# A 2-D Fourier mixing and maxout feed-forward kernel: the work before its first matrix products put in another order

## The chip, the cores and the metric

The kernel runs on one core of a Trainium2 chip. The metric is the device time of one execution in microseconds (us), lower is better. A few terms: TensorE (PE) multiplies matrices and writes to PSUM; VectorE (DVE), ScalarE (ACT) and GpSimd (POOL) work elementwise, and DVE and ACT clear PSUM ("eviction"); SP only issues DMAs, ACT and POOL also do. Each engine takes its instructions strictly in order.

## The reference

```python
X = np.fft.fft(np.fft.fft(x, axis=1), axis=2).real      # x: 8 x 3072 x 256
t = X.reshape(24576, 256)
h = np.maximum(np.maximum(t @ w1, t @ w2), t @ w3)      # 256 -> 768
out = h @ w_out                                         # 768 -> 256
```

## The kernel before, in words

**Tiling.** Each of the 8 batches has 3072 rows of 256. The Fourier transform is done as matrix products with tables of sines and cosines. A batch is held as 96 partitions (24 row blocks times 4 column groups) by 128 x 64 elements; a row index `bb` goes from 0 to 127. Products pair row `bb` with row 128-`bb`, so a second, reversed copy of the batch is needed (`reverse`, L125). The mixing of a batch (class `Mix`, L370) has seven stages `s` (L378; 66 products of up to 96 columns, each stage evicted into `z`), six stages `k` (L401; four products of 256 columns with `tabs`, evicted into `t`) and `end` (L421). Then 18 "units" (L687), each a 512-row block by one of six weight chunks: four products `unit_plus` (L427), two `unit_minus` (L437, executed after the next unit's four), and `unit_out` (L444), in which ACT makes a relu and DVE a maximum. The last products (`l2_block`, L461) run ten steps per unit, one block behind.

**Weights.** They are multiplied by the column transform first. `prep_first(jh, ...)` (L324) makes `gE`, `gO` and `gD` for half `jh` of the 768 columns: for each of two weight matrices it yields twice, each time after four products of 384 columns in one PSUM bank. `gE` and `gO` are evicted by copies, `gD` by ACT from the same PSUM bank with the scale `dif` (L341). `prep_second` (L345) makes `g1t` in three steps and `gw` in a fourth.

**The beginning (L156 to L320).** The raw batch 0 comes in six pieces. Rows 80 to 95, 96 to 111 and 112 to 127 are loaded as float32 into `staged` buffers by SP, ACT and SP (L160 to L168), each in four DMAs; the last piece also gets row 128 by `load_next` (L103), eight DMAs, issued after its four. Rows 0 to 31, 32 to 63 and 64 to 79 are loaded by POOL straight into `x0_first` as bfloat16 (L187 to L190). DMAs reuse eight completion counters per path, so a ninth DMA waits for the first to land. POOL writes index vectors first (`iota`, L156), and after the loads it issues the weights (L195, L200).

DVE builds first the small 24-point table (L229 to L263), of which ACT takes sines (L256) and small copies (L268); then the angles of the large table in two parts of 7 and 6 rows (L274 to L282): one pass for the product and three for the reduction to one turn (`_reduce`, L20). ACT takes four passes over each part (L284 to L287: sine, negative sine, absolute value, cosine) into `tabs`. DVE then casts the three `staged` pieces into `x0_first` (L293), and ACT makes the reversed copy `back` (L295, L312; DVE the small part at L313). DVE makes the 256-point angles `vm` (L301 to L309) and ACT their sines `md_all`, `nmd_all` (L310, L311).

**Order by hand.** The schedule is manual: the program's order is each engine's order. PE runs 14 warm-up products on the table (`warm`, L582), the seven `s` of batch 0 (with eviction by ACT, and by DVE for k = 1, 3, 5), `prep_first(0)`, `k0`, one step of `prep_first(1)`, `k1`, another step, and then the units. The dictionary `plan` (L621 to L660) says after which unit each remaining step runs: steps of the weights, the mixing of batch b+1 from unit `begin[b]` on (L640), POOL's reversed copies of the next batches (`turn_chunk`, L134: two casts for each of four chunks) and SP's loads (`fetch`, L635). While `prep_first(0)` and `k` run, the PSUM pool `ps_f` has two banks and `ps_s` six.

Of the kernel before, what the change touches and what calls it, by code (L numbers as in the profile page):

```python
# [9 lines left out]
FP32 = mybir.dt.float32  # L10
# [23 lines left out]
def kernel(  # L34
# [68 lines left out]
    def load_next(eng, dst, b, after=None):  # L103

        xr = x_rows(b)
        for g in range(4):
            for (a0, n, a) in ((0, 23, 1), (23, 1, 0)):
                ld = eng.dma_start(out=dst[g * 24 + a0: g * 24 + a0 + n],
                                   in_=xr[g, a:a + n, 0:1, :])
                if after is not None:  # L110
                    tc.add_manual_dep(ld.ins, after.ins.name, AFTER, reason="weights first")
# [44 lines left out]
    def iota(t, pattern, base=0, cm=0):  # L156
        nc.gpsimd.iota(t, pattern, base=base, channel_multiplier=cm,
                       allow_small_or_imprecise_dtypes=True)

    staged = []  # L160
    for (r0, eng) in ((80, nc.sync), (96, nc.scalar), (112, nc.sync)):
        n = 17 if r0 == 112 else 16
        xs = xs_pool.tile([96, 33 * 64], FP32, name="xs", tag="xs")
        xv = xs[:, 0:n * 64].rearrange("p (bb dl) -> p bb dl", dl=64)
        load_rows(eng, xv[:, 0:16, :], 0, r0, r0 + 16)
        if n > 16:
            load_next(eng, xv[:, 16:17, :], 0)
        staged.append((r0, n, xs))  # L168

    pidx = gen.tile([128, 1], FP32, tag="pidx")  # L170
    iota(pidx, [[0, 1]], cm=1)
    jm24 = gen.tile([96, 48], FP32, tag="jm24")
# [6 lines left out]
    i13 = gen.tile([128, 13], FP32, tag="i13")  # L179
    iota(i13, [[1, 13]])  # L180
    j128 = gen.tile([128, 128], FP32, tag="j128")
    iota(j128, [[24, 128]])
# [3 lines left out]

    x0_first = x0_pool.tile([96, 64 * 130], BF16, name="x0", tag="x0")  # L187
    x0v = x0_first.rearrange("p (bb dl) -> p bb dl", dl=64)
    for (r0, r1) in ((0, 32), (32, 64), (64, 80)):
        load_rows(nc.gpsimd, x0v[:, r0:r1, :], 0, r0, r1)  # L190
# [21 lines left out]
    nc.gpsimd.memset(z[:, :, 24:26], 0.0)  # L212

    consts_of = {}
    for (name, value) in (("half_pi", 0.5 * math.pi), ("rnd", ROUND), ("n24", -24.0),
                          ("n256", -256.0), ("n3072", -3072.0)):
# [3 lines left out]
    s24 = gen.tile([96, 24], FP32, tag="s24")  # L220
    nc.vector.memset(s24[:, 0:13], 6.0)
    nc.vector.memset(s24[:, 13:24], 0.0)
# [5 lines left out]

    ge24 = gen.tile([96, 5], FP32, tag="ge24")  # L229
# [27 lines left out]
    pi13 = gen.tile([128, 13], FP32, tag="pi13")  # L257
    nc.vector.tensor_scalar(out=pi13, in0=i13, scalar1=pidx, scalar2=None, op0=ALU.mult)
# [11 lines left out]
    w = gen.tile([128, 13 * 128], FP32, tag="w")  # L270
    v = gen.tile([128, 13 * 128], FP32, tag="v")
    q = gen.tile([128, 13 * 128], FP32, tag="q")
    turn = float(2.0 * math.pi / 3072.0)
    for (r0, r1) in ((0, 7), (7, 13)):  # L274
        cs = slice(r0 * 128, r1 * 128)
        n = r1 - r0
        nc.vector.scalar_tensor_tensor(
            out=v[:, cs].rearrange("p (r j) -> p r j", j=128),
            in0=j128.unsqueeze(1).to_broadcast([128, n, 128]), scalar=pidx,
            in1=pi13[:, r0:r1].unsqueeze(2).to_broadcast([128, n, 128]),  # L280
            op0=ALU.mult, op1=ALU.add)
        _reduce(nc, w[:, cs], v[:, cs], q[:, cs], 3072.0, consts_of["rnd"], consts_of["n3072"])  # L282
        wr = w[:, cs].rearrange("p (r j) -> p r j", j=128)
        nc.scalar.activation(out=tabs[:, r0:r1, 0, :], in_=wr, func=AX.Sin, scale=turn)  # L284
        nc.scalar.activation(out=tabs[:, r0:r1, 2, :], in_=wr, func=AX.Sin, scale=-turn)
        nc.scalar.activation(out=w[:, cs], in_=w[:, cs], func=AX.Abs)
        nc.scalar.activation(out=tabs[:, r0:r1, 1, :], in_=wr, func=AX.Sin, scale=-turn,  # L287
                             bias=consts_of["half_pi"])

    back = gen.tile([96, 33 * 130], BF16, tag="back")  # L290
    xr0 = back.rearrange("p (dl bb) -> p dl bb", bb=130)
    for (r0, n, xs) in (staged[1], staged[0], staged[2]):
        nc.vector.tensor_copy(out=x0_first[:, r0 * 64:(r0 + n) * 64], in_=xs[:, 0:n * 64])  # L293
    for (r0, n) in ((80, 49), (0, 31), (31, 32)):
        reverse(nc.scalar.copy, xr0, x0_first[:, r0 * 64:(r0 + n) * 64], r0, n)  # L295
# [3 lines left out]
    pf = gen.tile([128, 2], FP32, tag="pf")  # L299
    for fc in range(2):  # L300
        nc.vector.tensor_scalar(out=pf[:, fc:fc + 1], in0=pidx, scalar1=float(128 * fc),  # L301
                                scalar2=None, op0=ALU.add)
# [6 lines left out]
    _reduce(nc, vm, vm, qm, 256.0, consts_of["rnd"], consts_of["n256"])  # L309
    nc.scalar.activation(out=md_all, in_=vm, func=AX.Sin, scale=float(2.0 * math.pi / 256.0))  # L310
    nc.scalar.activation(out=nmd_all, in_=vm, func=AX.Sin, scale=float(-2.0 * math.pi / 256.0))  # L311
    reverse(nc.scalar.copy, xr0, x0_first[:, 63 * 64:80 * 64], 63, 17, 32, 49)  # L312
    reverse(nc.vector.tensor_copy, xr0, x0_first[:, 63 * 64:80 * 64], 63, 17, 49, 65)  # L313
# [10 lines left out]
    def prep_first(jh, evict_e, bank=lambda: ps_f.tile([128, 512], FP32, name="psg", tag="ps")):  # L324

        cs = slice(jh * 384, (jh + 1) * 384)
        for i, wv in enumerate((w2_bf, w3_bf)):
            for half in range(2):
                psg = bank()
                hs = slice(half * 128, (half + 1) * 128)  # L330
                for k, (table, wt) in enumerate(((md, wv), (nmd, w1_bf))):
                    for fc in range(2):
                        nc.tensor.matmul(  # L333
                            psg[:, 0:384], table[fc][:, hs],
                            wt[:, fc * DFF + jh * 384: fc * DFF + jh * 384 + 384],
                            start=(k == 0 and fc == 0), stop=(k == 1 and fc == 1))
                if half == 0:
                    evict_e(out=gE[i][:, cs], in_=psg[:, 0:384])
# [31 lines left out]
    class Mix:  # L370
# [30 lines left out]
        def k(self, q):  # L401
# [15 lines left out]
            nc.scalar.copy(  # L417
# [163 lines left out]
    for _ in range(14):  # L581
        nc.tensor.matmul(warm, tab[:, 4864:4992], tab[:, 4480:4992], start=True, stop=True)  # L582
# [5 lines left out]
    for _ in prep_first(0, nc.scalar.copy):  # L588
        pass
# [7 lines left out]
    second = [prep_first(1, nc.vector.tensor_copy,  # L597
                         lambda: ps_o.tile([128, 512], FP32, name="psg", tag="po")),
# [9 lines left out]

    m.k(0)
    prep_some()  # L610
    m.k(1)
    prep_some()
# [27 lines left out]
    begin = [8, 6] + [5] * (B - 3)  # L640

    for (u, fn) in ((0, prep_some), (1, prep_some),
                    (2, lambda: m.k(2)), (2, prep_some), (3, lambda: m.k(3)),
                    (3, prep_some), (4, prep_some), (5, prep_some),
                    (6, lambda: m.k(4)), (7, lambda: m.k(5)), (7, m.end),
                    (0, lambda: turn_chunk(1, 0)), (2, lambda: turn_chunk(1, 1)),
                    (4, lambda: turn_chunk(1, 2)), (6, lambda: turn_chunk(1, 3))):
        at(0, u, fn)
    for ch in range(4):
        at(0, (3, 5, 7, 9)[ch], lambda ch=ch: fetch(2, ch))  # L650
    for b in range(B - 1):
        for i, whats in enumerate(ahead):
            for what in whats:
                at(b, begin[b] + i, lambda b=b, what=what: piece(b + 1, what))
        if b + 2 < B:
            folds = begin[b] + 8
# [79 lines left out]
```

## Time and profile before

| | us |
|---|---|
| median of 3 runs | 435.25 (434.59 to 435.59) |
| the profiled execution's own time | 436.12 |
| its span, first to last instruction | 434.3 |
| PE busy | 405.1 (93% of the span) |
| DVE, ACT, POOL busy | 273.7, 264.7, 240.1 |
| mean granted TensorE clock | 0.992 |

The profiled execution has 1.8 us outside the span. The page gives for each engine its busy time, then groups of instructions by line; the trace can be asked for rows in order of time: start, duration, engine, line, operation, output<-inputs, and in brackets how long the engine was idle before and what ended that. "x4" is several instructions in one row. PEq, SPq and so on are the sequencers, which issue DMAs.

### The profile page before, as it was taken

What the parts mean: (1) busy time and instruction counts of PE and PEld (TensorE: products, weight loads), DVE (VectorE), ACT (ScalarE), POOL (GpSimd) and SP (SyncE); (2) the same over time, 40 slices, a digit from 0 to 9 for tenths busy, and PEclk for the clock granted to TensorE, in tenths of its full rate; (3) what the DMA queues carried; (4) which work ended last, traced back from release to release, by engine and by line L of the source; (5) the groups of instructions that cost most, each with busy time, mean ns of one, the idle gap of its engine ahead of it and who ended that gap; (6) DMA issues with size and microseconds to landing.
All of it is one profiled execution on the core that took longest, in us unless ns stands there. A gap on an engine that the chain in (4) does not pass through costs nothing.

```text
span 434.3 us, 8699 instructions
## 1 busy us (share of the span) xinstructions
PE 405.1 (93%) x3015; PEld 271.7 (63%) x3070; DVE 273.7 (63%) x449; ACT 264.7 (61%) x486; POOL 240.1 (55%) x288
## 2 busy tenths in 40 slices
PE   0479999998999999999999999999999999999996
PEld 0165666666666666766666666666666666666665
DVE  8724755666656666666656756576656666666773
ACT  3877666665666576656665566656665666754650
POOL 8718522698258922995259823994269812214320
PEclk9969999999999999999999999999999999999999
DMA  9998774176424953188415854186421221111313
GB/s 140 135 180 172 145 185 117 62 188 164 120 74 124 220 115 109 52 205 184 131 50 127 195 121 129 58 197 163 130 76 67 75 62 72 74 50 49 101 72 122
DMA packets 130180, 52.28 MB, mean 120 GB/s; under 512 B 112081, under 2 KB 127192, under 8 KB 130136
## 3 DMA queue, kind: packets, MB, share of 16 engines
q1 hardware_dynamic: 107784, 36.52, 35.3%
q0 software_dynamic: 20624, 14.68, 14.7%
q10 hardware_dynamic: 1728, 0.52, 0.5%
q8 instruction: 24, 0.39, 0.4%
q14 instruction: 20, 0.16, 0.1%
HBM read 29.02 MB, written 25.17 MB: 125 GB/s over the span
## 4 chain that ended last, share of the span: by engine, by line
PE 81%; issue 4%; DVE 4%; POOL 3%; ACT 3%; DMA 3%; DVEq 0%; POOLq 0%; ACTq 0%
PE po L457 26%; PE pse L433 14%; PE pse L441 12%; PE pse L434 11%; PE po L481 3%; PE ps L389 2%; PE ps L387 2%; PE ps L413 2%; PE ps L415 2%; PE pl L473 2%; ACT stmp L447 2%; DMA x<-in_x_dram 2%; DVE ot L486 2%; DVE hm L448 1%; PE psg L333 1%
## 5 line engine op out<-in xcount | busy, mean ns | idle before, releaser
L447 ACT ACTIVATE stmp<-pse 128x512 bf16<-128x512 f32 x288 | 171.1, 600 | 52.4 <-PE pse L434 38.1
L491 POOL DMA_INDIRECT out_dram<-ot,rows_m x92 | 100.3, 1090 | 169.6 <-DVE ot L486 155.2
L448 DVE TENSOR_TENSOR hp<-pse,stmp 128x512 bf16<-128x512 f32 x144 | 99.5, 691 | 130.9 <-ACT stmp L447 95.7
L433 PE MATMUL pse<-t,gE 128*128 128x512 bf16 x287 | 108.8, 379 | 2.6 <-DVE hm L448 0.4
L448 DVE TENSOR_TENSOR hm<-pse,stmp 128x512 bf16<-128x512 f32 x144 | 99.2, 689 | 7.0 <-PE pse L434 3.9
L434 PE MATMUL pse<-t,gO 128*128 128x512 bf16 x256 | 96.9, 379 | 0.1
L457 PE MATMUL po<-wout_bf,hp 128*128 128x256 bf16 x576 | 86.1, 273 | 0.4
L441 PE MATMUL pse<-t,gD 128*128 128x512 bf16 x273 | 82.4, 379 | 0.4
L457 PE MATMUL po<-wout_bf,hm 128*128 128x256 bf16 x576 | 78.5, 273 | 0.3
L457 PEld LDWEIGHTS <-hp 128*128 128x128 bf16 x576 | 56.4, 98 | 26.1
L457 PEld LDWEIGHTS <-hm 128*128 128x128 bf16 x576 | 56.4, 98 | 16.3
L486 DVE TENSOR_TENSOR ot<-po,even 128x512 f32<-128x512 f32 x92 | 62.9, 683 | 0.2 <-PE po L457 0.2
L143 POOL CAST x<-xs 96x1056 bf16<-96x1056 f32 x28 | 56.7, 2025 | 11.1 <-DMA xs<-in_x_dram 11.1
L145 POOL CAST x<-xs 96x1056 bf16<-96x1056 f32 (+1 forms) x35 | 58.1, 1670 | 0.0
L417 ACT CAST t<-ps 128x512 bf16<-128x512 f32 x48 | 28.1, 585 | 43.5 <-PE ps L415 42.2
L394 ACT CAST z_all<-ps 128x480 bf16<-128x480 f32 x45 | 25.1, 558 | 44.3 <-PE ps L389 40.1
L441 PEld LDWEIGHTS <-gD 128*128 128x128 bf16 x288 | 27.9, 98 | 32.2
L434 PEld LDWEIGHTS <-gO 128*128 128x128 bf16 x288 | 28.1, 98 | 21.0 <-issue 3.0
L433 PEld LDWEIGHTS <-gE 128*128 128x128 bf16 x288 | 28.1, 98 | 19.2 <-issue 0.4
L481 PE MATMUL po<-gw,t 128*128 128x512 bf16 x85 | 32.2, 379 | 0.0
L387 PE MATMUL ps<-m24f,x 96*128 96x96 bf16 (+1 forms) x256 | 30.3, 214 | 0.0
L477 ACT COPY even<-pl 128x512 f32<-128x512 f32 x46 | 26.8, 583 | 0.0
(133 smaller groups left out, 326.4 us busy)
## 6 DMA issues: line engine op xcount, KB each, us to landing
xs<-in_x_dram SPq DMA_DIRECT2D x84, 198.0 KB
out_dram<-ot SPq DMA_DIRECT2D x90, 128.0 KB
xs<-in_x_dram SPq DMA_DIRECT2D x28, 192.0 KB
out_dram<-ot,rows_m POOLq DMA_INDIRECT x92, 4.5
w_bf<-in_moe_w_dram POOLq DMA_DIRECT2D x6, 192.0 KB, 6.0
out_dram<-ot SPq DMA_DIRECT2D x17, 64.0 KB
xs<-in_x_dram SPq DMA_DIRECT2D x8, 96.0 KB
x<-in_x_dram POOLq DMA_DIRECT2D x8, 96.0 KB, 8.3
```

What stands on the lines that cost most here:

```text
L143: nc.gpsimd.tensor_copy(v[:, 0:33, ch * 32:ch * 32 + 32], xs[:, 0:32 * 64].rearrange("p (bb dl) -> p dl bb", dl=64)[:, 0:33, :])
L145: reverse(lambda out, in_: nc.gpsimd.tensor_copy(out, in_), v[:, 33:66, :], xs, ch * 32, 33 if ch == 3 else 32)
L387: nc.tensor.matmul(ps1[:, c0:c0 + n], x0[0](d), mf[:, 0:n], start=True, stop=False)
L433: nc.tensor.matmul(pse[:, 0:n], gE[i][:, js], te, start=True, stop=False)
L434: nc.tensor.matmul(pse[:, 0:n], gO[i][:, js], to, start=False, stop=True)
L441: nc.tensor.matmul(pse, gD[i][:, js], to, start=False, stop=True, skip_group_check=True)
L447: nc.scalar.activation(out=stmp[:, 0:n], in_=pses[0][:, 0:n], func=AX.Relu)
L448: nc.vector.tensor_tensor(out=dst, in0=src3, in1=stmp[:, 0:n], op=ALU.max)
L457: nc.tensor.matmul(po, hcols(jc), wout_bf[:, jc * 256:(jc + 1) * 256], start=False, stop=(jc == NJC - 1), skip_group_check=True)
L481: nc.tensor.matmul(po, to[:, cp], gw[:, 256:768], start=True, stop=True)
L486: nc.vector.tensor_tensor(out=ot.rearrange("p (h c) -> p h c", h=2), in0=po.rearrange("p (h c) -> p h c", h=2), in1=lin.unsqueeze(1).to_br ...
L491: stored(nc.gpsimd.indirect_dma_start(out, bass.IndirectOffsetOnAxis(ap=rows_m[0:128 - lo, b * 12 + slot: b * 12 + slot + 1], axis=0), ot[ ...
```

## The change

The reading, the mathematics and the sizes stay. What changes, in the order of the program:

- `load_next` issues five DMAs in place of eight, and for batch 0 it goes ahead of the bulk of rows 112 to 127 on SP.
- POOL writes only `pidx`, `j128` and `i13` before its first four loads of `x0_first`; the other index vectors are put between the loads. The memset of two columns of `z` goes from POOL to DVE.
- The large table comes first on DVE and ACT, and its angles are counted in turns: one product pass and two reduction passes (the first with one source) in place of one and three. ACT makes three passes in place of four; the negative sine is made by DVE (`tab_minus`), for the first seven rows before `vm`, for the last six after all copies. The 24-point table follows.
- `vm` is reduced in two passes in place of three, `half` is set twice, and `nmd_all` is made by DVE from `md_all`.
- ACT reverses the three `staged` pieces straight from float32, before DVE's casts; row pieces 31 to 62 are reversed by DVE. ACT keeps a 48-element strip (which waits for the casts), rows 0 to 30, and half of rows 63 to 79.
- 17 warm-up products in place of 14, on the first rows of the table.
- `prep_first` uses the six-bank pool in the beginning; `gE` is always evicted by DVE, `gD` is made by POOL from `gO`. The order on PE is: seven `s`, two steps of `prep_first(0)`, `k0`, `k1` (evicted by DVE), the other two steps, and then unit 0; the four steps of `prep_first(1)` follow after units 0, 0, 1 and 1.
- The mixing of batch 1 begins after unit 10 in place of 8 (its last seven steps one unit earlier than that would give), two of batch 1's `turn_chunk` go from units 4 and 6 to 5 and 8, the loads of batch 2 from units 3, 5, 7, 9 to 6, 7, 9, 11, and the `turn_chunk` of batch 2 from 16, 18, 20, 22 to 14, 16, 18, 20.

```diff
+        if n > 16:
+            load_next(eng, xv[:, 16:17, :], 0)
         load_rows(eng, xv[:, 0:16, :], 0, r0, r0 + 16)
...
+        nc.vector.tensor_scalar(out=q[:, cs], in0=v[:, cs], scalar1=ROUND, scalar2=None,
+                                op0=ALU.add)
+        nc.vector.scalar_tensor_tensor(out=w[:, cs], in0=q[:, cs], scalar=-ROUND, in1=v[:, cs],
+                                       op0=ALU.add, op1=ALU.subtract)
...
+    tab_angles(0, 7)
+    tab_sines(0, 7)
+    tab_angles(7, 13)
+    tab_sines(7, 13)
...
-    for (r0, n, xs) in (staged[1], staged[0], staged[2]):
-        nc.vector.tensor_copy(out=x0_first[:, r0 * 64:(r0 + n) * 64], in_=xs[:, 0:n * 64])
-    for (r0, n) in ((80, 49), (0, 31), (31, 32)):
-        reverse(nc.scalar.copy, xr0, x0_first[:, r0 * 64:(r0 + n) * 64], r0, n)
+    for (r0, n, xs) in staged:
+        nc.vector.tensor_copy(out=x0_first[:, r0 * 64:(r0 + n) * 64], in_=xs[:, 0:n * 64])
+        reverse(nc.scalar.copy, xr0, xs, r0, n, 32, 64)
+    nc.scalar.activation(out=md_all, in_=vm, func=AX.Sin, scale=float(-2.0 * math.pi / 256.0))
+    for (copy, r0, n, d0, d1) in ((nc.scalar.copy, 80, 49, 64, 65),
+                                  (nc.scalar.copy, 0, 31, 32, 65),
+                                  (nc.vector.tensor_copy, 31, 32, 32, 65),
+                                  (nc.scalar.copy, 63, 17, 32, 49),
+                                  (nc.vector.tensor_copy, 63, 17, 49, 65)):
+        reverse(copy, xr0, x0_first[:, r0 * 64:(r0 + n) * 64], r0, n, d0, d1)
+    nc.vector.tensor_scalar(out=nmd_all, in0=md_all, scalar1=-1.0, scalar2=None, op0=ALU.mult)
+    tab_minus(7, 13)
...
-                    nc.scalar.activation(out=gD[i][:, cs], in_=psg[:, 0:384], func=AX.Copy,
-                                         scale=dif)
+                    nc.gpsimd.tensor_scalar(out=gD[i][:, cs], in0=gO[i][:, cs], scalar1=dif,
+                                            scalar2=None, op0=ALU.mult)
...
-    for _ in prep_first(0, nc.scalar.copy):
+    first = prep_first(0, lambda: ps_s.tile([128, 512], FP32, name="psg", tag="ps"))
+    next(first)
+    next(first)
+    m.k(0)
+    m.k(1, nc.vector.tensor_copy)
+    for _ in first:
         pass
...
-    begin = [8, 6] + [5] * (B - 3)
+    begin = [10, 6] + [5] * (B - 3)
```

More of the change, by code (lines that the diff above doesn't have):

```diff
@@ L105, in load_next @@
         xr = x_rows(b)
[L106 to L111, printed above, removed]
+        parts = [(dst[g * 24: g * 24 + 23], xr[g, 1:24, 0:1, :]) for g in range(4)]
+        parts.append((dst[23:96:24], xr[:, 0, 0:1, :]))
+        for (to, src) in parts:
+            ld = eng.dma_start(out=to, in_=src)
+            if after is not None:
+                tc.add_manual_dep(ld.ins, after.ins.name, AFTER, reason="weights first")
     def load_chunk(b, ch, after=None):
@@ L268 @@
             nc.scalar.activation(out=m[:, o0:o1], in_=src, func=AX.Copy, scale=by)
[L270 to L291, printed above, removed]
-    for (r0, n, xs) in (staged[1], staged[0], staged[2]):
-        nc.vector.tensor_copy(out=x0_first[:, r0 * 64:(r0 + n) * 64], in_=xs[:, 0:n * 64])
-    for (r0, n) in ((80, 49), (0, 31), (31, 32)):
-        reverse(nc.scalar.copy, xr0, x0_first[:, r0 * 64:(r0 + n) * 64], r0, n)
+    tab_minus(0, 7)
     vm = gen.tile([128, 512], FP32, tag="vm")
@@ L308 @@
                                 scalar1=128.0, scalar2=64.0, op0=ALU.mult, op1=ALU.add)
[L309 to L313, printed above, removed]
+    nc.vector.tensor_scalar(out=qm, in0=vm, scalar1=256.0 * ROUND, scalar2=None, op0=ALU.add)
+    nc.vector.scalar_tensor_tensor(out=vm, in0=qm, scalar=-256.0 * ROUND, in1=vm,
+                                   op0=ALU.add, op1=ALU.subtract)
+    back = gen.tile([96, 33 * 130], BF16, tag="back")
+    xr0 = back.rearrange("p (dl bb) -> p dl bb", bb=130)
+    for (r0, n, xs) in staged:
[10 more added lines that the diff above has]
+    tab_minus(7, 13)
     nc.vector.tensor_scalar(out=sgn, in0=pidx, scalar1=0.0, scalar2=None, op0=ALU.is_equal)
@@ L580 @@
     warm = ps_s.tile([128, 512], FP32, name="warm", tag="ps")
-    for _ in range(14):
-        nc.tensor.matmul(warm, tab[:, 4864:4992], tab[:, 4480:4992], start=True, stop=True)
+    for _ in range(17):
+        nc.tensor.matmul(warm, tab[:, 0:128], tab[:, 0:512], start=True, stop=True)
     m = Mix(0)
@@ L653 @@
             for what in whats:
-                at(b, begin[b] + i, lambda b=b, what=what: piece(b + 1, what))
+                at(b, begin[b] + i - (b == 0 and i >= 6), lambda b=b, what=what: piece(b + 1, what))
         if b + 2 < B:
-            folds = begin[b] + 8
+            folds = begin[b] + 8 if b else 14
             for ch in range(4):
```

83 lines of the change are left out of this document (53 added, 30 removed).

## The prediction, written before the changed kernel was run

> **What bounds the kernel now.** I read the table of waits first, for PE alone over the whole span (engine, line, what it waited for, us in total, times, longest).
>
> ```profile
> PE warm L582 <- ACT tab L287: 17.1, 1, 17.1
> PE ps L389 <- ACT back L130: 2.8, 1, 2.8
> PE ps L389 <- POOL x L145: 1.3, 1, 1.3
> ```
>
> PE stands still for 17.1 us, warms up, stands still for 2.8 us more until ACT's reversed copy is done, and after that hardly waits. So the end is set by two things: when the first real product can run, and how fast PE then goes through a fixed list of products. The change touches the first, and a little of the second. Next, the two engines that make what PE waits for, in order of time: first ACT, then DVE.
>
> ```profile
> 4.52 0.28 ACT L256 ACTIVATE t<-v 96x96 f32<-96x96 f32 x1 [0.52 <-DVE v L30]
> ...
> 5.83 0.30 ACT L268 ACTIVATE m0r<-t,ind 96x24 bf16<-96x24 f32 x1
> 9.73 0.95 ACT L284 ACTIVATE tab<-w 128x896 bf16<-128x896 f32 x1 [3.59 <-DVE w L30]
> ...
> 13.63 0.84 ACT L284 ACTIVATE tab<-w 128x768 bf16<-128x768 f32 x1
> ...
> 18.07 6.84 ACT L130 COPY back<-x 96x1568 bf16<-96x1568 bf16 x4 [1.02 <-DVE x L293]
> ```
>
> ```profile
> 1.56 0.65 DVE L230 TENSOR_SCALAR ge<-g,pidx 96x5 f32<-96x5 f32 x1
> ...
> 4.83 0.25 DVE L260 TENSOR_TENSOR m24f<-t,ind 96x96 bf16<-96x96 f32 x1 [0.20 <-ACT t L256]
> ...
> 5.18 1.14 DVE L277 SCALAR_TENSOR_TENSOR v<-j,pidx,pi 128x896 f32<-128x896 f32 x1
> ...
> 9.61 1.01 DVE L277 SCALAR_TENSOR_TENSOR v<-j,pidx,pi 128x768 f32<-128x768 f32 x1
> ...
> 13.52 1.43 DVE L293 CAST x<-xs 96x1024 bf16<-96x1024 f32 x2
> 17.31 0.72 DVE L293 CAST x<-xs 96x1088 bf16<-96x1088 f32 x1 [2.36 <-DMA xs<-in_x_dram]
> 17.96 0.14 DVE L301 TENSOR_SCALAR pf<-pidx 128x1 f32<-128x1 f32 x1
> ...
> 21.94 0.41 DVE L130 COPY back<-x 96x272 bf16<-96x272 bf16 x1
> ```
>
> The reader sees a chain: ACT begins the reversed copy only at 18.07, when DVE has cast the third staged piece, and that piece was late (DVE idle 2.36 us at 17.31). Then four copies in a row take 6.84 us, to 24.91, and the first `s` runs at 24.97. Then PE's clock, by stretches (length, busy PE, PEld, DVE, ACT, POOL, then the granted clock), and three rows of PE in time.
>
> ```profile
> 24.97:30.07 5.10, 5.10 (x65) 5.10 (x66) 1.48 (x3) 3.14 (x6) 0.00 (x0) 0.50 1.04 180
> 30.07:36.26 6.19, 5.85 (x34) 3.47 (x33) 1.05 (x2) 4.21 (x10) 3.99 (x2) 0.91 0.70 158
> 57.52:57.95 0.43, 0.43 (x13) 0.43 (x11) 0.21 (x1) 0.00 (x0) 0.41 (x2) 1.00 0.92 210
> 102.74:106.15 3.41, 3.36 (x34) 2.38 (x36) 1.73 (x3) 1.66 (x4) 2.79 (x3) 1.00 0.58 133
> ```
>
> ```profile
> 39.07 0.49 PE L333 MATMUL psg<-w_bf,md_all 128*128 128x384 bf16 x2
> 39.39 0.49 PE L333 MATMUL psg<-w_bf,nmd_all 128*128 128x384 bf16 x2
> 39.72 0.38 PE L433 MATMUL pse<-t,gE 128*128 128x512 bf16 x1
> ```
>
> All seven `s` of batch 0 run at clock 0.50, in 5.10 us; one `s` of batch 1 takes 0.43 us at 1.00. Four `psg` products take 0.65 us at full clock (39.07 to 39.72). Unit 0 begins where the second stretch ends, at 36.26.
>
> **The change, part by part.** *DVE up to the 24-point table.* A two-source pass over the large table is 4.43/4 = 1.11 us for seven rows (5.18 to 9.61), 6/7 of that for six. The new first reduction pass has one source; the trace has none on float32 alone. The nearest row is the single-source cast, 1.43/2 for 1024 elements, so 0.63 for 896; from the other side it is a full pass, 1.11. I take 0.63. Beginning at about 2.1 (the first small operation of before ends at 2.21), rows 0 to 6 are ready at 2.1 + 1.11 + 0.63 + 1.11 = 4.95, rows 7 to 12 at 7.4. The 24-point chain takes 1.56 to 4.52 = 2.96, so its angles are ready at 10.4.
>
> *ACT.* Four passes took 13.63 - 9.73 = 3.90; three take 2.9 and 2.5. ACT is through at 7.9 and 10.4, takes the sine (0.28) and small copies (to 6.13 from 4.52, 1.6) and is free at about 12.0. Reversed copies cost 6.84 us for 1568 + 48 + 1023 + 1056 = 3695 elements, 1.85 ns each; the three staged pieces, 512, 512 and 544 elements from float32, then take 2.9 us by that row. From above I allow twice, since no row reverses float32. ACT reaches 14.9 and makes `md_all`, then waits for DVE's casts.
>
> *DVE to the end of the casts.* The 24-point products, 4.83 to 5.18, with the wait for ACT end at 11.2; the negative sine of 896 elements is 0.63 by the cast's row (bounds half of it, as both sides are bfloat16, and 1.11), to 11.8. `half` twice, 0.3. The `vm` chain took 21.94 - 17.96 = 3.98; it loses one of three passes of 512 elements (1.11 x 512/896 = 0.63) and 0.27 of another: 3.1, to 15.2. Three casts of 0.72: 17.35.
>
> *The critical end.* ACT's 48-element strip waits for the third cast: 17.7 with its overhead (0.3). Rows 0 to 30: 1023 x 1.85 = 1.9, so 19.6. DVE beside it makes 1056 + 272 elements, by 0.41/272 at most 2.0 us: 19.4. The first `s` runs at about **19.6 instead of 24.97, 5.4 us earlier**. With every unknown at its dear end (three passes 0.48, 0.41 and 0.48 longer, `vm` 0.27) it is 21.2; with the cheap end 19.3. What is late next is that strip behind the casts, and after it the data: the third piece no longer has the small transfers behind it.
>
> ```profile
> 6.45 6.52 SPq L108 DMA_DIRECT2D xs<-in_x_dram  x8
> ```
>
> These eight are issued from 6.45 to 12.97, waiting for counters of bulk loads; now five go out when the first counters are free, and the bulk of rows 112 to 127 goes about 3 us later than before. DVE needs it at 16.6, after two casts. In before DVE waited for the last of the eight until 17.31; the bulk itself had landed before the last of the eight was issued (12.97), so 3 us later is about 16, still ahead of 16.6, so I cost the move at nothing, covered by the `vm` chain. Should it land at 17.3 again, the start is 0.7 later.
>
> *POOL's loads.* Three index vectors fewer stand ahead of them, so each issue comes about 0.9 us earlier; the rows of the last four are needed at about 18.9.
>
> ```profile
> 12.52 0.68 POOL L99 DMA_DIRECT2D x<-in_x_dram  x1 [1.69 <-DMA x<-in_x_dram]
> 13.40 1.06 POOL L99 DMA_DIRECT2D x<-in_x_dram  x1 [0.21 <-issue]
> ```
>
> ```profile
> x<-in_x_dram POOLq DMA_DIRECT2D x4, 48.0 KB, 4.8
> ```
>
> In before the last issue ends at 14.46; with 4.8 us to land, these rows come by 18.4 to 19.3, now up to 0.9 earlier: just hidden. Here the issue beside DVE's casts took 1.06, the one before it, beside two-source passes, 0.68. The Trainium skill, "SBUF — State Buffer", section "Who interferes with whom", says that copies and single-source operations of VectorE in their two-port modes lock GpSimd out for the whole instruction, descriptor writing included, which speaks against the change, since its reduction passes become such. The two rows agree in direction, at 0.38 us per issue that meets one. By the rows that is at most 12 x 0.38 = 4.6 us, below as rival C; in the sum I take nothing, since only three such passes run between 2 and 12 us.
>
> *The clock.* Warm-up starts when the negative sine is written, at 11.8.
>
> ```profile
> 17.11 5.06 PE L582 MATMUL warm<-tab 128*128 128x512 bf16 x14 [17.11 <-ACT tab L287]
> ```
>
> Seventeen take 5.06 plus three at 0.21 to 0.43, so they end at 17.5 to 19.0 and the gap to 19.6 is 0.6 to 2.1 us. In before a gap of 2.8 lost the clock (0.50 from 24.97), a gap of 1.3 did not (1.00 after 102.74). I take it as kept: seven `s` at 0.43 (the last shorter) are 2.8 instead of 5.1, and the 6.19 us at 0.91 that follow hold 0.09 x 6.19 = 0.55 of lost clock: **2.8 us**. The Trainium skill, "TensorE: Matmul & The Clock Gate", "What's actually happening", puts the fall after an idle window of about 3.4 us; the gap of 2.8 above lost it, so the trace is stricter, and by the page rival B would have no chance.
>
> *Between `s` and unit 0.* From 30.07 to 36.26 PE did 24 `psg` (3.9) and two `k` (8 products of 256 columns, by columns 0.87 at 0.65 per 4 x 384) plus the 0.55: 0.87 us were waits for two PSUM banks. Six banks and DVE's share remove about **0.8**; the evictions of `s` keep up, four of them on ACT at 0.56 in 2.8 us.
>
> ```profile
> L394 ACT CAST z_all<-ps 128x480 bf16<-128x480 f32 x45 | 25.1, 558 | 44.3 <-PE ps L389 40.1
> ```
>
> The eight `psg` that move behind units 0 and 1 cost the same there.
>
> *Units.* `gD` on POOL: the fourth one stands behind the two casts of the next batch's first chunk.
>
> ```profile
> 31.88 1.99 POOL L143 CAST x<-xs 96x1056 bf16<-96x1056 f32 x1 [9.14 <-DMA xs<-in_x_dram]
> 33.81 2.06 POOL L145 CAST x<-xs 96x1056 bf16<-96x1056 f32 x1
> ```
>
> They start when their data lands, which nothing in the change hastens, and end at 35.87. 384 elements cost 0.36 (a fifth of a cast) to 2.0; by the cast's rate 0.75, so ready at 36.7. PE needs it after unit 4's first four products: 19.6 + 2.8 + 3.5 = 25.9, plus units of 1.3 (six products of 512 columns, by columns) and the moved steps (2.2 + 2.6 + 2.2 + 2.2) and 0.9 is 35.9. **A new wait of 0.8 us** (0 with a late start, 2 at most). ACT loses those passes; it was not on the path.
>
> *Batches 1 and 2.* Batch 2's reversed copies go two units earlier, so the wait of 1.3 us for POOL, just ahead of 102.74, goes: **1.3**. Batch 1's last chunk was through at 49.9; now it has a store ahead of it and ends at about 51.
>
> ```profile
> 47.72 2.19 POOL L145 CAST x<-xs 96x1056 bf16<-96x1056 f32 x2
> ```
>
> It is needed after unit 10, six units of at least 2.4 us (1.3 and ten last steps) after unit 4's 35.9, so at 50.3, and about 53 with the steps between (`psw`, `k4`, `k5`): covered by a us or two, and the first `s` of batch 1 is where a wait would show.
>
> Sum: 5.4 + 2.8 + 0.8 + 1.3 - 0.8 = **9.5 us**. The profiled execution took 436.12, so 426.6; that execution is 0.87 above the median of 435.25, so against the median **425.8**.
>
> **The rivals.** *B, the clock is lost in the gap.* Then the 2.8 is not won, some 0.3 of the bank waits stays, and PE reaches the fourth `gD` 3 us later, so the 0.8 is not paid: 5.4 + 0.5 + 1.3 = 7.2, time 428.0. For it: the gap of 2.8; against: that of 1.3.
>
> *C, the start is later than 19.6* because POOL's issues are locked out or passes are dear. From 21.2 (by the passes) to 14.46 - 0.9 + 4.6 + 4.8 + 0.4 = 23.4 (by the issues), and with the longer gap the clock goes too: gain 3.8 + 1.8 = 5.6 down to 1.6 + 1.8 = 3.4: 429.7 to 431.9. For it: 1.06 against 0.68; against: earlier issues.
>
> *D, slower: the fourth `gD` waits.* POOL is in order, so PE's fifth unit waits for the next batch's first chunk. The wait is 0.8 us plus each us by which that chunk lands after 31.9. Without the wait the gain is 10.3, so it turns at a landing of 41.4, 9.5 us late; at 44 the time is 437.9. For it: the loads wait for weights that share POOL's queue; against: nothing adds bytes.
>
> *E, nothing:* the start is bound by data in both kernels, so that only batch 2's wait is won or even less: 434 to 435.3. Against it: after 18.07 PE waits for 6.84 us of copies, not for DMA.
>
> **How the numbers follow.** Forecast 0.48, B 0.27, C 0.15, D 0.04, E 0.06 (0.04 of it within 0.2%, 0.02 slower). A measurement of this kernel tells about 0.2%, 0.87 us, from no change. Faster 0.90, same 0.04, slower 0.06. The range goes from 423.5 (start at 19.2, no wait for `gD`, one more us of waits gone) to 431.0 (most of C); outside it are half of C, D and E, and little below.
>
> **What would show it.** Right: first `s` near 19.6, PEclk 1.00 from there, seven `s` in under 3.5 us, unit 0 near 26, no wait of PE for POOL near 103, one of below 2 us for `gD` near 36. Wrong: POOL issues above 1 us throughout, ACT's staged reversals near 2 us each, the strip (48 elements) starting after 18.5, a clock of 0.50 after 20, or batch 1's first `s` waiting for POOL.

## The result, and the profile after

| | before | after |
|---|---|---|
| median of 4 runs | 435.42 us (434.59 to 436.03) | 429.27 us (428.13 to 429.83) |
| the profiled execution's own time | 436.12 | 428.75 |
| its span | 434.3 | 427.0 |
| mean granted TensorE clock | 0.992 | 0.994 |

The ratio is 0.986, with a 95% interval of 0.983 to 0.989: faster by 1.4%. The forecast of 425.8 is 3.5 us too low; the range (423.5 to 431.0) holds the time, since it was laid to take in rival B and most of C. Between the two profiled executions the gain is 7.4 us, where the sum said 9.5.

PE's waits after, as they stood for before (line, what was waited for, us in total, times, longest):

```profile
PE warm L610 <- DVE tab L258: 11.7, 1, 11.7
PE ps L415 <- DMA w_bf<-in_moe_w_dram: 2.0, 1, 2.0
PE ps L417 <- ACT back L130: 0.7, 1, 0.7
PE pse L461 <- ACT gO L368: 0.6, 1, 0.6
PE po L548 <- DVE ot L554: 0.5, 1, 0.5
```

The wait for POOL is gone. One of 0.6 for `gO` has come. Of the 17.1 us before the warm-up 11.7 are left. (The second row names a weight's DMA; the first `s` reads `x`, whose last rows DVE waits for until 19.31, below.) PE, then ACT, then DVE, in order of time at the start:

```profile
16.80 0.81 PE L610 MATMUL warm<-tab 128*128 128x512 bf16 x3
19.65 0.26 PE L415 MATMUL ps<-m24f,x 96*128 96x96 bf16 x1 [2.04 <-DMA w_bf<-in_moe_w_dram]
20.65 0.22 PE L417 MATMUL ps<-m24r,back 96*128 96x96 bf16 x1 [0.73 <-ACT back L130]
```

```profile
12.01 2.04 ACT L130 CAST back<-xs 96x512 bf16<-96x512 f32 x2
16.88 1.18 ACT L130 CAST back<-xs 96x544 bf16<-96x544 f32 x1 [2.82 <-DMA xs<-in_x_dram]
17.96 0.63 ACT L333 ACTIVATE md_all<-vm 128x512 bf16<-128x512 f32 x1
18.49 2.69 ACT L130 COPY back<-x 96x48 bf16<-96x48 bf16 x3
```

```profile
2.88 0.98 DVE L244 TENSOR_SCALAR q<-v 128x896 f32<-128x896 f32 x1
...
11.15 0.41 DVE L258 TENSOR_SCALAR tab<-tab 128x896 bf16<-128x896 bf16 x1
...
16.88 0.72 DVE L331 CAST x<-xs 96x1088 bf16<-96x1088 f32 x1 [0.88 <-DMA xs<-in_x_dram]
...
19.31 0.40 DVE L130 COPY back<-x 96x272 bf16<-96x272 bf16 x1 [0.24 <-DMA x<-in_x_dram]
```

ACT is free at 14.05 and stands until 16.88, because the next copy in its order needs the third staged piece. What comes behind it (`md_all`, rows 0 to 30) needs nothing from that piece. So the `s` start in earnest at 20.65, although DVE has its last rows at 19.31. The clock, over the seven `s` and then up to unit 0 (length, busy PE, PEld, DVE, ACT, POOL, clock):

```profile
20.65:25.36 4.71, 4.71 (x66) 4.71 (x67) 1.50 (x4) 2.20 (x4) 2.23 (x7) 0.72 1.18 161
25.36:29.96 4.60, 4.04 (x26) 2.62 (x25) 2.27 (x4) 1.88 (x5) 1.25 (x1) 0.91 1.15 190
```

PE pauses from 17.61 to 20.65 with one product in it. The clock falls at 22.76, for 3.4 us, in the middle of the `s`. The seven `s` take 4.71 us in place of 5.10. That is 1.9 us more than forecast, and only partly for the clock, since PEld (weight loads) is busy through all of the stretch:

```profile
L415 PEld LDWEIGHTS <-x 96*128 96x128 bf16 x16 | 2.2, 171 | 0.0
L417 PEld LDWEIGHTS <-back 96*128 96x128 bf16 x16 | 2.1, 140 | 0.9 <-ACT back L130 0.9
```

These are the loads from 20.6 to 22.7, at clock 1.00 (count, then busy us and mean ns): 171 ns from `x`, 140 from `back`. This is what the experiments take up.

### The profile page after: what moved, and what is told of

Read it like the earlier page. It is cut to its first block, busy times and chain, and to the rows that moved or that the text cites. A ratio compares the mean times of both kernels' runs of the same rounds, so it can differ in the third digit from the quotient of the medians.

```text
span 427.0 us, 8732 instructions
## 1 busy us (share of the span) xinstructions
PE 407.5 (95%) x3073; PEld 271.5 (64%) x3073; DVE 274.1 (64%) x455; ACT 258.1 (60%) x477; POOL 244.3 (57%) x291
## 4 chain that ended last, share of the span: by engine, by line
PE 94%; POOL 2%; DMA 2%; ACT 1%; DVE 0%; issue 0%; POOLq 0%
PE po L485 29%; PE pse L461 15%; PE pse L462 15%; PE pse L469 14%; PE po L509 5%; PE ps L415 3%; PE ps L417 3%; PE ps L443 3%; PE ps L441 2%; PE pl L501 2%; POOL x L99 2%; DMA x<-in_x_dram 2%; PE psg L361 1%; ACT back L130 0%; PE pst L380 0%
## 5 line engine op out<-in xcount | busy, mean ns | idle before, releaser
L462 PE MATMUL pse<-t,gO 128*128 128x512 bf16 x288 | 109.0, 378 | 0.0
L469 PE MATMUL pse<-t,gD 128*128 128x512 bf16 x288 | 85.6, 379 | 0.0
L509 PE MATMUL po<-gw,t 128*128 128x512 bf16 x92 | 34.9, 379 | 0.0
L415 PEld LDWEIGHTS <-x 96*128 96x128 bf16 x264 | 25.3, 106 | 3.0 <-DVE back L130 2.5
```

Of the source, the lines that this page charges most:

```text
L415: nc.tensor.matmul(ps1[:, c0:c0 + n], x0[0](d), mf[:, 0:n], start=True, stop=False)
L462: nc.tensor.matmul(pse[:, 0:n], gO[i][:, js], to, start=False, stop=True)
L469: nc.tensor.matmul(pse, gD[i][:, js], to, start=False, stop=True, skip_group_check=True)
L509: nc.tensor.matmul(po, to[:, cp], gw[:, 256:768], start=True, stop=True)
```

## The experiments

Each kernel shares its chip with runs of the kernel before. Those medians were 436.31, 435.45 and 435.71 us in the three groups, so ratios compare across groups and times only within one. The ratio is that of the mean times, among the experiments without the profiled execution, so it isn't the quotient of the two medians. "Clock" is the mean granted clock of a kernel's runs, lowest to highest.

| kernel | median us | ratio to before (95%) | clock |
|---|---|---|---|
| changed kernel | 429.27 | 0.9857 (0.9828 to 0.9886) | 0.991 to 0.996 |
| e_fill | 428.94 | 0.9826 (0.9805 to 0.9848) | 0.990 to 1.000 |
| e_warm | 430.79 | 0.9853 (0.9830 to 0.9876) | 0.991 to 0.996 |
| e_contig | 428.44 | 0.9811 (0.9793 to 0.9829) | 0.994 to 1.000 |
| e_plan | 430.36 | 0.9873 (0.9853 to 0.9892) | 0.990 to 0.996 |
| e_bulk | 429.34 | 0.9860 (0.9838 to 0.9881) | 0.992 to 0.996 |
| e_fillwarm | 427.11 | 0.9829 (0.9803 to 0.9856) | 0.991 to 1.000 |
| e_gdact | 430.51 | 0.9891 (0.9874 to 0.9908) | 0.990 to 0.994 |
| f_prep | 427.39 | 0.9814 (0.9800 to 0.9829) | 0.998 to 1.000 |
| f_contig | 426.58 | 0.9794 (0.9776 to 0.9813) | 0.998 to 1.000 |
| f_bank | 427.45 | 0.9818 (0.9801 to 0.9834) | 0.998 to 1.000 |

My theory after the result: the start is late because ACT stands behind the third piece, and the `s` are slow because of the stride in their weights, more than because of the clock. The rivals: the data sets the start; the clock is the price.

**e_fill: what ACT could do while it waits.**

```diff
     for (r0, n, xs) in staged:
         nc.vector.tensor_copy(out=x0_first[:, r0 * 64:(r0 + n) * 64], in_=xs[:, 0:n * 64])
+        if r0 == 112:
+            nc.scalar.activation(out=md_all, in_=vm, func=AX.Sin, ...)
+            reverse(nc.scalar.copy, xr0, x0_first[:, 0:31 * 64], 0, 31)
         reverse(nc.scalar.copy, xr0, xs, r0, n, 32, 64)
-    nc.scalar.activation(out=md_all, in_=vm, func=AX.Sin, ...)
...
-                                  (nc.scalar.copy, 0, 31, 32, 65),
```

> The changed kernel with ACT's order altered: md_all and the reversed copy of rows 0 to 30 go ahead of the third staged piece. Theory 1 (ACT, strictly in order, stands 2.82 us behind the late third piece, and this sets the first product that reads back at 20.65): ACT fills the wait, ends md_all at 15.2, rows 0 to 30 at 17.2, the third piece at 18.4, the strip at 18.7, and rows 63 to 79 at 19.7, when their data has landed; the first product on back comes at 19.75, 0.9 us earlier, and the time is 0.9 below the changed kernel, about 428.4. Theory 2 (the data of rows 63 to 79, which DVE waits for until 19.31, sets the start, and ACT only happens to end late): the first product on back stays within 0.2 us of 20.65 and the time at 429.3. If the clock is also kept, because the pause of PE is 2.0 us and not 3.0, up to 0.4 us more.

ACT of this kernel, in order of time:

```profile
15.19 1.94 ACT L130 COPY back<-x 96x1023 bf16<-96x1023 bf16 x1
17.37 1.16 ACT L130 CAST back<-xs 96x544 bf16<-96x544 f32 x1 [0.25 <-DMA xs<-in_x_dram]
18.44 0.27 ACT L130 COPY back<-x 96x48 bf16<-96x48 bf16 x1
19.81 0.69 ACT L130 COPY back<-x 96x289 bf16<-96x289 bf16 x1 [1.10 <-DMA x<-in_x_dram]
```

The wait of 2.82 us is down to 0.25, and ACT now waits for the data of rows 63 to 79, like DVE. In this run these rows came later (DVE's last copy begins at 19.72, not 19.31). The first product on `back` follows that copy's begin by 0.53 us (20.25), in place of 1.34: 0.8 us won. The ratio falls by 0.003, about as much, but the intervals overlap. Theory 1 holds by the trace (the time alone wouldn't show it), and behind it the data is the bound. The clock fell in this run all the same, for 6.8 us; in one run of five it did not (1.000, 427.66 us).

**e_warm, e_fillwarm: the pause and the clock.** `range(17)` became `range(26)`, alone and together with the edit of e_fill.

> The changed kernel with 26 warm-up products in place of 17. Nine more at 0.21 us end at 19.5, so PE pauses for 1.1 us with one product in it, in place of 3.0. Theory 1 (the seven s of batch 0 are held by the loading of their weights, which took 0.066 us a product at clock 1.00 and 0.071 at 0.50, so that the lost clock costs little): the granted clock stays 1.00 through the s, they take 4.3 to 4.5 us in place of 4.71, the psg products behind gain some 0.2, and the time falls by 0.4 to 0.6 us, to about 428.8. Theory 2 (the term of the prediction: the clock is the price, and the seven s take 2.8 us at 1.00): the time falls by 1.9 us or more, to 427.4. Theory 3 (the clock falls all the same): no change.

> The changed kernel with ACT's wait filled (md_all and rows 0 to 30 ahead of the third staged piece) and 26 warm-up products, so that PE pauses only 0.2 to 0.8 us before the s of batch 0. Theory 1 (the pause loses the clock, as the prediction had it): the clock stays 1.00 through the s in every run, mean clock 0.998 or more, they take 4.3 to 4.5 us, and the time is 1 to 2 us below that of the kernel with the filled wait alone (ratio to the kernel before 0.979 in place of 0.983). Theory 2 (the s of batch 0 themselves lose it, because PE spends 40% of the time on loading weights there: 67 ns a product for 40 ns of columns): the clock still falls for 3.4 or 6.8 us, mean clock 0.991 to 0.996, ratio 0.983.

First the kernel with more warm-ups alone, in stretches of 3.41 us up to and after the fall, then the one with both edits, over its `s`:

```profile
15.93:19.34 3.41, 3.41 (x17) 1.47 (x15) 1.85 (x2) 2.09 (x4) 2.20 (x3) 1.00 1.16 129
19.34:22.75 3.41, 2.19 (x28) 1.89 (x28) 1.58 (x8) 2.77 (x3) 3.19 (x7) 1.00 1.03 139
22.75:26.16 3.41, 3.41 (x44) 3.24 (x43) 1.55 (x3) 1.24 (x4) 0.60 (x2) 0.50 1.27 169
26.16:29.57 3.41, 3.41 (x14) 1.97 (x13) 0.70 (x2) 0.86 (x4) 0.40 (x1) 0.50 1.08 189
```

```profile
19.75:24.08 4.33, 4.33 (x66) 4.33 (x66) 2.25 (x8) 1.93 (x4) 3.04 (x8) 1.00 1.19 173
```

More warm-ups alone do nothing (its theory 3): with waits of 0.31 and 0.91 us left, PE is busy for 64% of the 3.41 us before 22.75, and the clock falls, for 6.8 us. With ACT's wait filled as well, PE waits 0.28 us ahead of the `s`, the clock stays at 1.00, and four of five runs lie at 426.90 to 427.33 with a mean clock of 0.999 or 1.000; the fifth lost it (0.991, 429.62). So closing the pause keeps the clock: a mean of 0.998 or more was kept by 13 of 14 runs of e_fillwarm, f_bank and f_prep, and by 3 of 33 runs of the kernels that leave the pause (one of e_fill, two of e_contig). The run of e_fillwarm that lost it was 2.5 us longer. But at full clock the `s` still take 4.33 us, not 2.8.

The length of a pause alone doesn't decide: 1.33 us in the kernel before (at 102.74) did not lose the clock. Nor does PE's busy share. In each trace the changes of the clock lie whole multiples of 3.41 us apart, so the trace can be cut into stretches of that length. In the changed kernel the clock held through one with PE busy for 49% (15.93 to 19.35, warm-ups) and fell after one with 70% (19.35 to 22.76, mostly `s`). An estimate separates them better: count each product by its columns alone, at 0.04 us for 96 (from 0.65 us for four of 384 at full clock), which leaves out what the strided load adds to an `s` product. By that count the stretches before a fall are filled to 39% at most in the fourteen traces, and those through which the clock held to 42% or more, but for one of 37% at a run's end. It fits what was recorded; no run was made to try it. By it the pause and the stride lost the clock together. The Trainium skill, "TensorE: Matmul & The Clock Gate", section "What's actually happening", lets the clock fall after an idle window of about 3.4 us. The length agrees with the falls seen here (3.4 and 6.8 us); the condition doesn't: no window ahead of 22.75 was idle.

**e_contig, f_contig: the stride.** One line, in the changed kernel and in e_fillwarm. Both then multiply other elements than the transform needs, so they serve for the time alone:

```diff
-    x0f = (lambda d: x0v[:, 0:128, d], rows_back(xr0))
+    x0f = (lambda d: x0_first[:, d * 128:(d + 1) * 128], rows_back(xr0))
```

> The changed kernel, but the forward products of the seven s of batch 0 read 128 neighbouring elements of the first copy instead of every 64th; the products are the same in number and size, their values are not the transform's. Theory 1 (the stride of 64 elements in the loaded weights makes a load 171 ns in place of 97, and PE's weight loads are 100% busy in this stretch): a load takes about 97 ns as in batch 1, the seven s take 66 x 0.035 = 2.3 us at full clock, at most 3.0, in place of 4.71, and the time falls by 1.7 to 2.4 us, to about 427.2. Theory 2 (the half clock, or the evictions, hold them): the s stay above 4 us and the time within 0.5 us of 429.3.

> The kernel with the filled wait and 26 warm-up products, with the forward products of the seven s of batch 0 reading neighbouring elements in place of every 64th (the values are not the transform's). Here the clock should hold, so that the stride is seen alone. Theory 1 (the strided weight load is what holds the s at 67 ns a product): a product takes 33 to 40 ns at clock 1.00, the seven s 2.2 to 2.8 us in place of 4.3, and the time is 1.5 to 2.1 us below that of the kernel without the edit; the prediction's 2.8 us for the s comes true. Theory 2 (the evictions by ACT and DVE hold them, four of 0.56 and three of 0.66 us on two engines): the s stay above 3.5 us.

The first one's clock fell as its `s` began (at 20.63; they took 4.30 us), so its trace can't show the stride apart from the clock; only its ratio is lower (the intervals just touch). The second kernel, where the clock holds: loads, then the stretch of its `s`.

```profile
L418 PEld LDWEIGHTS <-back 96*128 96x128 bf16 x33 | 2.8, 98 | 0.1
L416 PEld LDWEIGHTS <-x 96*128 96x128 bf16 x32 | 2.7, 98 | 0.0
```

```profile
20.34:23.00 2.66, 2.66 (x67) 2.66 (x66) 1.73 (x6) 1.53 (x3) 2.42 (x6) 1.00 1.23 176
```

A load from `x` falls from 171 to 98 ns, those from `back` that alternate with it from 140 to 98, and the seven `s` from 4.33 to 2.7 us. So theory 1: the stride costs 1.7 us at full clock. The time, however, falls by 0.8 to 0.9 against f_prep and f_bank on the same chip (426.58 to 427.39 and 427.45; the intervals overlap), not by 1.5 to 2.1. A new wait shows where most of the rest went in the profiled execution; PE, then POOL:

```profile
38.95 0.39 PE L470 MATMUL pse<-t,gD 128*128 128x512 bf16 x1 [1.31 <-POOL gD L370]
```

```profile
33.68 2.01 POOL L143 CAST x<-xs 96x1056 bf16<-96x1056 f32 x1 [2.30 <-DMA xs<-in_x_dram]
35.63 2.05 POOL L145 CAST x<-xs 96x1056 bf16<-96x1056 f32 x1
37.64 1.25 POOL L370 TENSOR_SCALAR gD<-gO,dif 128x384 bf16<-128x384 bf16 x1
```

This is the wait of the prediction's `gD` term: the fourth `gD` behind chunk 0 of batch 1, which waits for its load. It appears as soon as PE comes early enough.

**e_plan: the units.** `begin`, `turn_chunk`, `fetch` and `folds` as in the kernel before.

```diff
-    begin = [10, 6] + [5] * (B - 3)
+    begin = [8, 6] + [5] * (B - 3)
...
-            folds = begin[b] + 8 if b else 14
+            folds = begin[b] + 8
```

> The changed kernel with the plan of the kernel before for the units: batch 1 begins after unit 8, its reversed copies stand at units 0, 2, 4 and 6, the loads of batch 2 at 3, 5, 7 and 9, its reversed copies at 16, 18, 20 and 22. Theory 1 (POOL's wait of 1.3 us near 102 vanished because batch 2's copies go two units earlier): a wait of PE for POOL of about 1.3 us comes back between 95 and 103, and the time is 1.3 to 1.9 us above the changed kernel, 430.6 to 431.2. Theory 2 (the wait vanished because the beginning ended earlier): no wait for POOL there, time within 0.4 us of 429.3. Theory 3 (begin after unit 8 meets the unfinished chunk 3 of batch 1 at about 52 to 56): a wait of PE for POOL near 50 of 2 to 4 us, and a time of 431 or more.

```profile
95.26 0.21 PE L415 MATMUL ps<-m24f,x 96*128 96x96 bf16 x1
96.84 0.22 PE L417 MATMUL ps<-m24r,x 96*128 96x96 bf16 x1 [1.37 <-POOL x L145]
```

The wait is back, 1.37 us, at the first `s` of batch 2: theory 1. The ratio is 0.0016 higher (0.7 us), with overlapping intervals. Near 50 no wait for POOL came (against theory 3).

**e_bulk: the order on SP.** `load_next` behind the bulk of rows 112 to 127, still in five transfers.

> The changed kernel with SP issuing the bulk of rows 112 to 127 first and the five small transfers of row 128 behind it. Theory 1 (the third staged piece landed at 16.88, 2.82 us late for ACT, because its bulk stands behind five small transfers that wait for counters): the piece is there by 15.5, ACT waits for it under 1.5 us, and the first product that reads back comes about 0.9 us sooner after the landing of rows 64 to 79 than in the changed kernel (0.4 in place of 1.3 us after DVE starts its last copy); time 0.5 to 1.0 us lower. Theory 2 (the transfers share engines that are busy all the time, so one piece is hastened at the cost of another): the third piece lands earlier, rows 64 to 79 later by as much, and the time does not move. Theory 3 (row 128 is what comes last, as in the kernel before): the piece still lands at 16.5 to 17.5 and nothing changes.

```profile
16.85 1.16 ACT L130 CAST back<-xs 96x544 bf16<-96x544 f32 x1 [2.80 <-DMA xs<-in_x_dram]
```

16.85 in place of 16.88, the same time: theory 3 (theory 2 would have had it earlier). The order of these transfers is worth nothing here; in the eight traces in which ACT stood waiting for the piece, its cast began between 16.56 and 17.37.

**e_gdact: `gD` on ACT again**, by the two removed lines of the diff.

> The changed kernel with gD made by ACT from PSUM again, in place of POOL from gO. Theory 1 (moving gD off ACT is worth something): four passes of about 0.5 us come back on ACT between the evictions of gO and t, unit 0 waits longer than the 0.57 us for gO, and the time rises by 0.3 to 0.8 us. Theory 2 (ACT has room there, and POOL's 1.24 us each were hidden): no change beyond 0.3 us, and chunk 0 of batch 1 is cast from about 32 instead of 34.1. Theory 3 (the fourth gD on POOL costs a wait, as the prediction had it): 0.8 us faster.

```profile
PE pse L461 <- ACT gD L369: 1.1, 1, 1.1
```

The wait ahead of unit 0 grows from 0.57 to 1.05, chunk 0 is cast from 31.96 on, and the ratio rises by 0.0034, some 1.5 us (theory 1, with intervals that overlap a little). Half a microsecond is that wait. The rest is not placed; all five runs here had a clock of 0.990 to 0.994, and in the trace it fell for 6.8 us in place of 3.4, so part of it may be the clock.

**f_bank, f_prep: between the `s` and unit 0.** Both on e_fillwarm: `prep_first(0)` in the two-bank pool, and one step of `prep_first(1)` ahead of unit 0.

> The kernel with the filled wait and 26 warm-up products, with prep_first(0) in the two-bank PSUM pool again in place of the six-bank pool. Theory 1 (the prediction's 0.8 us between the s and unit 0 come from the banks): waits of PE for the evictions of psg and t come back, 0.5 to 0.9 us in all between the end of the s and unit 0, which took 4.2 us here, and the time rises by as much. Theory 2 (they come from the order and the engines, with two steps, two k and two steps in place of four steps): waits below 0.3 us, no change.

> The kernel with the filled wait and 26 warm-up products, and besides one of the four steps of prep_first(1) (four products, 0.65 us) put ahead of unit 0 in place of behind it. Theory 1 (PE stands 0.57 us before unit 0 until ACT has evicted the last gO, and any work that is ready fills it): the wait vanishes, unit 0 is done with no delay, and everything behind is 0.5 to 0.6 us earlier: ratio to the kernel before about 0.9815 where the clock holds, time 8.0 to 9.0 us below it. Theory 2 (the step ahead of unit 0 waits for a PSUM bank, or ACT then evicts one more gO ahead of the first relu and the wait comes back behind unit 0): no change against the kernel without it.

With two banks PE takes 4.06 us from the `s` to unit 0, with six 4.21:

```profile
24.39:28.45 4.06, 3.95 (x27) 2.49 (x26) 2.20 (x4) 1.45 (x4) 1.25 (x1) 1.00 1.17 185
```

```profile
24.08:28.29 4.21, 3.64 (x28) 2.47 (x27) 2.25 (x4) 1.89 (x5) 1.25 (x1) 1.00 1.19 181
```

With two banks gaps of 0.17, 0.13 and 0.27 us stand between the steps (theory 1 has these right), but the wait of 0.57 ahead of unit 0 is gone, and the time is the same as in f_prep. In f_prep that wait stands ahead of the step that was put there:

```profile
28.64 0.48 PE L362 MATMUL psg<-w_bf,md_all 128*128 128x384 bf16 x2 [0.57 <-ACT gO L369]
```

So whatever product comes first into the pools that follow waits for the last `gO`, and work put there doesn't fill the wait (theory 2 of f_prep, in its outcome). That it is the bank of that `gO` which is waited for agrees with both runs, but it wasn't tried apart.

**e_probe, f_probe: the price of the single-source float32 pass.** Six such passes of 896 elements behind `tab_minus(7, 13)` in the changed kernel, and four behind the first angles in e_fillwarm.

> The changed kernel with six more single-source float32 passes of 896 elements on DVE, into a buffer that nothing reads later, from about 20.2 on. Theory 1 (the first reduction pass took 0.98 us, not 0.63, because POOL issued transfers beside it): the first passes, beside POOL's issues, take 0.95 to 1.0 us each, and those after 23.2, when POOL is idle, about 0.65 to 0.72, the rate of the 0.43 us that 512 elements took beside an idle POOL. Theory 2 (the float32 pass costs this always, the cast's rate was the wrong row): all six take 0.95 to 1.0. The time rises by under 4 us in both, since two evictions wait.

> The kernel with the filled wait and 26 warm-up products, with four more single-source float32 passes of 896 elements on DVE right behind the first three table passes, from about 4.9 on; they write a buffer that is written again later. The same pass took 0.98 us at 2.88 and 0.61 to 0.63 at 20.1 to 23.6. Theory 1 (it is dear beside POOL's issues of the loads of batch 0, which cover 1.5 to 5.1 and 5.6 to 8.8): the passes beside them take 0.95 to 1.0, any that lies in the index vectors from 5.1 to 5.6 or behind the issues 0.6 to 0.8. Theory 2 (it was dear because it reads what the pass ahead of it has just written): all four take 0.6 to 0.65. The time of the run rises by up to 4 us by the longer beginning.

Each was run once (429.59 and 429.95 us). Duration in ns (least, median, most) of the six, then of the four:

```profile
L343 DVE TENSOR_SCALAR q<-v x6: 607/628/799, 20.1 to 23.6; 128x896 f32<-128x896 f32 x6
```

```profile
L263 DVE TENSOR_SCALAR q<-v x4: 627/711/807, 5.0 to 7.2; 128x896 f32<-128x896 f32 x4
```

The same pass at 2.88 took 0.98. Neither theory holds as written: the first of the six took 0.61 in the middle of POOL's issues of weights, while among the four, two beside the issues of batch 0's loads took 0.79 and 0.81. The cast's rate (0.63) is what the pass costs undisturbed; what stretches it is open. In one case POOL's issue was longer instead: the second of the four took 0.63 beside an issue that took 1.14, where the next three issues took 0.81 to 0.85.

## Why the prediction was right and wrong, step by step

**The start: 4.3 us of the 5.4.** DVE's and ACT's chains came nearly as summed: warm-up at 11.71 (11.8 forecast), ACT's first reversed copy at 12.01 (12.0). The first reduction passes took 0.98 and 0.84 (0.63 and 0.54); an earlier begin (1.70 for 2.1), a shorter 24-point chain (2.6 for 2.96) and `tab_minus` (0.41 for 0.63) gave that back. That the casts were done at 17.60 (17.35 forecast) is luck: DVE was through with two at 16.00 and waited 0.88 us for the third piece. The step that failed is the one behind "I cost the move at nothing, covered by the `vm` chain". It put the landing of the third piece at about 16 and asked when DVE needs it (16.6). It was there only at 16.88, and ACT, which goes in order, was ready for it at 14.05, so that a landing at 16 would have stopped it too. The move itself did cost nothing (e_bulk); not putting the free copies ahead of the wait cost 0.8 (e_fill). Had ACT not stood there, the data would have set about 19.8 (in e_fillwarm the first product on `back` came at 19.75).

**The clock: the term of 2.8 us was the largest error, and two things were wrong in it.** It was lost, as rival B had it, though later, in the `s`, for 3.4 us: a gap was judged by its length alone, 2.8 against 1.3. And "seven `s` at 0.43" took batch 1's row for batch 0, whose first copy lies row by row, so that its weight loads read every 64th element. At full clock the `s` take 4.33, so the whole clock was worth 0.8 us there and not 2.3 (e_fillwarm), and only with neighbouring elements do they take 2.7 (f_contig). The changed kernel won 0.39.

**Banks: 0.8 forecast, about 0.3 found.** Before, 6.19 us less the eight `psg` that moved (1.3) is 4.89; after, 4.60. The clock was 0.91 in both. Six banks take away one set of waits and bring the one of 0.57 (f_bank).

**The wait for the fourth `gD`: -0.8 forecast, nothing found.** Its price was 1.24 and not 0.75, and the casts ahead of it began at 34.09, not 31.88: the third `gD` stands before them on POOL, which the prediction left out. But PE came only at 40.02 (35.9 forecast), when it had been done since 39.3.

```profile
32.90 1.24 POOL L369 TENSOR_SCALAR gD<-gO,dif 128x384 bf16<-128x384 bf16 x1 [1.65 <-ACT gO L368]
34.09 2.00 POOL L143 CAST x<-xs 96x1056 bf16<-96x1056 f32 x1
38.07 1.24 POOL L369 TENSOR_SCALAR gD<-gO,dif 128x384 bf16<-128x384 bf16 x1
40.02 0.59 PE L469 MATMUL pse<-t,gD 128*128 128x512 bf16 x2
```

With the earlier start of f_contig it is there, 1.31 us: the mechanism was right, and rival D is what waits behind the next gain.

**Batch 2: 1.3 forecast, 1.33 found** in the PE waits, and e_plan brought it back. Batch 1's copies were covered, as forecast.

In sum rival B (428.0, gain 7.2 us) is nearest to what happened: clock lost, no `gD` wait, with a start 1.1 us later than B had. That its gain nearly equals the 7.4 us between the profiled executions is partly luck, since the parts found make only 6.3. Of the rest, 0.6 are two waits of unit products in the kernel before (0.26 for ACT at 152.43, 0.35 for DVE at 153.16), which the changed kernel's execution lacks and e_fill's shows again (0.66 and 0.24), so they are probably not the change's doing. By number C's near end (429.7) lies closer to the median, but not by its cause: the twelve issues of batch 0's loads took 0.68 to 1.06 us, as before. The median stands 0.5 above the profiled execution, whose clock (0.994) is the second best of the four runs: 428.13 at 0.996, 429.83 at 0.992.

**A better version** is e_fillwarm, with or without the edits of f_bank or f_prep: 427.1 to 427.5 us, some 8 us below before. Of its 14 runs 13 kept the clock, at 426.90 to 427.63; the changed kernel's runs lie at 428.13 to 429.83.

## What to carry to other kernels

When a transfer is moved, ask which engine in order comes to it first, and what ready work stands behind it there; that work belongs ahead of the wait. Take the price of a product from a row with the same layout of its operands, not only the same shape: here the stride of the loaded operand made the `s` 1.6 times as long (4.33 us for 2.66). Where a pause can cost the clock, close all of it, since closing a part (e_warm) brought nothing.

## What the runs showed of the hardware

- A strided read of the loaded operand (128 elements, 128 bytes apart) took 171 ns for 98, and the contiguous loads that alternate with it 140. At clock 0.50 it hardly shows in the products: before, 66 products (two pairs of them narrower) took 5.10 us, 0.077 each, and e_contig's contiguous ones came 0.08 apart at that clock.
- The clock fell after stretches of 3.41 us with PE busy for 64% (e_warm, waits of 1.2 us in all) and 70% (changed kernel), and held through one with 49%; the share that the columns fill (39% at most before a fall) separates them better, as an estimate. After the fall one stretch of 3.41 us with PE busy all the time did not always bring it back (the changed kernel after one, e_warm after two). What tells these two apart stayed open.
- POOL's product of 128 x 384 bfloat16 by a column took 1.24 us, against 0.59 for ACT's from PSUM (in e_gdact).
